# Where the operands of TensorE's matmuls begin in SBUF: weights at multiples of 64 bytes, moving operands 32 bytes past one

## The chip, the cores and the metric

The kernel runs on one core of a Trainium2 chip. The metric is the device time of one execution in microseconds (us): 1510.12 is the median of three runs of the kernel before (1508.47 to 1510.69). The profile is of one further execution, which took 1509.39 us, 1507.2 of them inside the span that the profiler shows.

## The reference

Two stages run one after the other, in float32. The first is an attention over 32 inducing points for each of 4 batches of 12416 tokens with 128 channels; the second is a gated feed-forward layer (SwiGLU) with 1536 hidden units over all 49664 tokens.

```
def mab(q, kv):
    s = scale * (q @ kv.transpose(0, 2, 1))
    a = softmax(s)                      # with 1e-9 in the divisor
    return a @ kv
h = mab(I, x)                           # I: the inducing points, for each batch
y = mab(x, h)
g = y @ w_gate                          # 128 x 1536
out = (g * sigmoid(g) * (y @ w_val)) @ w_out
```

## The kernel before, in words

Nearly all of the time is the feed-forward layer. Its input y is never formed: y = a @ h, so y @ w_gate = a @ (h @ w_gate), and the 32 rows of h @ w_gate and of h @ w_val are computed once for each batch and kept as the weight tile `tw` (128 partitions x 3072, float32r; the halves of a high-and-low split lie in different groups of 32 partitions). The attention weights a, split and transposed in the same way, are put into a tile `stack` (128 x 512 or 480) by small DMAs on SP's queue.

A batch is 25 column units of 512 or 480 tokens (for each, one `stack`), a unit is 12 slots, and a slot is 128 hidden units. In a slot TensorE runs five matmuls, each with 128 x 128 weights and 512 or 480 moving columns:

- `front`: L670 and L671, weights from `tw`, moving operand `stack`. ScalarE then takes silu of the gate (L673), and VectorE multiplies (L678) into `h`, or in place in PSUM for three slots of twelve.
- `split`: `h_hi` is h rounded to float32r (L687, ScalarE, in one slot of twelve VectorE), `h_lo` is the rest h - h_hi (L689, GpSimd, VectorE in three slots of twelve).
- `back`: L703 (weights `wo_lo`, moving `h_hi`), L704 (`wo_hi`, `h_hi`), L705 (`wo_hi`, `h_lo`), accumulated over the 12 slots of a unit in one PSUM bank.

The first unit of the first batch is an exception: its `back` is one plain float32 matmul (L701) on an unsplit h, which lies in a buffer of the `h_hi` pool; its weights stand in tiles called `s_all`, `tw` and `xn_sb`.

The order of all instructions is written out by hand (lists of steps with the slot at which each runs), so the scheduler moves nothing. The attention of the next batch is spread over the slots of the present one.

What the change touches is where tiles lie. A partition's bytes are handed out in the order in which pools are opened and tiles are named, each tile rounded up to 32 bytes. `stack`, `h_hi` and `h_lo` are allocated with `WF + SKIP` columns (WF = 512), of which 512 are used; they rotate through 3, 11 and 10 buffers. `odd` is a column of 0 and -1, allocated early, ahead of all weights. These are the addresses in the built programs, as the remainder by 64 bytes:

| tile | used as | before | after |
|---|---|---|---|
| `tw`, `wo_hi`, `wo_lo` | weights of L670, L671, L703 to L705 | 32 | 0 |
| `stack`, 3 buffers | moving, L670 and L671 | 32, 0, 32 | 32 |
| `h_hi`, 11 buffers | moving, L703 and L704 | 0, 32, 0, ... (six at 0) | 32 |
| `h_lo`, 10 buffers | moving, L705 | 32, 0, 32, ... (five at 0) | 32 |
| `silu`, `h`, `xn_sb` | ScalarE, VectorE, GpSimd; `xn_sb` moving in L306 | 0 | 32 |
| `xt_sb`, `eT`, `wgv_sb`, `a_hi`, `a_lo` | attention | 32 | 0 |
| `below` | weights of L399 | 0 | 32 |
| `s_all` of batches 0 and 2; of 1 and 3 | attention | 32; 0 (with L701's weights) | 32; 32 |

A weight slice begins a multiple of 512 bytes behind the start of its tile, so the remainder of a tile is that of all its slices.

Of the kernel before, what the change touches and what calls it, by code (L numbers as in the profile page):

```python
# [9 lines left out]
F32 = mybir.dt.float32  # L10
# [8 lines left out]
P = 128  # L19
# [13 lines left out]
NF = len(FC)  # L33
W = 32 * max(CH)
WF = 32 * max(FC)
SKIP = 8
NT = DFF // P
SCALE = 1.0 / math.sqrt(C)

# [70 lines left out]
def induced_set_attention_then_swiglu(ctx: ExitStack, tc: tile.TileContext, xt, xn, ind, wgv, wo, out):  # L110
    nc = tc.nc

    const = ctx.enter_context(tc.tile_pool(name="const", bufs=1))
# [4 lines left out]
    one = ctx.enter_context(tc.tile_pool(name="one", bufs=1))  # L118
# [14 lines left out]
    group = const.tile([P, NG], F32, name="group")  # L133
    nc.vector.tensor_reduce(out=group, in_=ident.rearrange("p (j m) -> p j m", m=M), op=ALU.add, axis=AX.X)

    odd = const.tile([P, 1], F32, name="odd")
    nc.gpsimd.memset(odd, 0.0)
    for j in (1, 3):
        nc.gpsimd.memset(odd[32 * j:32 * j + 32, :], -1.0)
# [59 lines left out]
    def attention(b, one, xn0=None, xt0=None):  # L199
# [266 lines left out]
        def stack(u):  # L466
            if u not in st.stack:
                st.stack[u] = stp.tile([P, WF + SKIP], F32R, name="stack")[:, :WF]
            return st.stack[u]
# [190 lines left out]
    def front(st, b, c, t):  # L660
# [13 lines left out]
        if u.whole:  # L674
            u.h = hip.tile([P, WF + SKIP], F32, name="h_hi")[:, :WF]
        else:
# [4 lines left out]
    def split(u):  # L681
        if u.whole:
            return
        n = u.n
        u.hi = hip.tile([P, WF + SKIP], F32R, name="h_hi")[:, :WF]
        u.lo = lop.tile([P, WF + SKIP], F32R, name="h_lo")[:, :WF]
        (nc.vector.tensor_copy if u.cast_dve else nc.scalar.copy)(out=u.hi[:, :n], in_=u.h[:, :n])  # L687
# [108 lines left out]
```

## Time and profile before

| | |
|---|---|
| median of three runs | 1510.12 us |
| the profiled execution | 1509.39 us |
| its span | 1507.2 us |
| TensorE busy | 1485.9 us (99%) |
| ScalarE busy | 1282.9 us (85%) |
| VectorE busy | 1219.0 us (81%) |
| GpSimd busy | 1207.1 us (80%) |
| matmuls of the five lines | 1200 each of L670 and L671, 1188 each of L703, L704 and L705 |

The granted TensorE clock is 9 of 10 tenths or more in every slice of the page. A busy TensorE is not yet one at its peak: matmuls overlap, and the next begins before the modelled end of the one ahead. The pace is therefore read from how many matmuls begin in a stretch without waits.

### The profile page before, as it was taken

The page shows a single profiled execution, that of the slowest core. Times are in us where ns is not written, and L with a number is a line of the kernel's source. Part 1 is how long each engine was busy: PE and PEld are TensorE (multiplying, and loading weights), DVE is VectorE, ACT ScalarE, POOL GpSimd, SP SyncE. Part 2 cuts the span into 40 slices and gives each one's busy share as a digit, 9 for nine tenths or more (in the row PEclk, how much of TensorE's full clock was granted, in tenths as well). Part 3 has the DMA queues.
Part 4 walks back from the last instruction along what each step waited for, and adds up shares of the span by engine and source line. Part 5 has one row for each costly group of instructions (what it writes and reads, how often), then busy time and mean ns, then how long its engine had stood idle before and what let it go on. Part 6 is the DMA issues. An engine that isn't in the chain of part 4 may idle for free.

```text
span 1507.2 us, 24960 instructions
## 1 busy us (share of the span) xinstructions
PE 1485.9 (99%) x7465; PEld 1167.9 (77%) x7465; DVE 1219.0 (81%) x2083; ACT 1282.9 (85%) x2389; POOL 1207.1 (80%) x995
## 2 busy tenths in 40 slices
PE   8899999999999999999999999999999999999999
PEld 5476777778887776788887777678888887888887
DVE  6788878878888778788888778878878878878877
ACT  4787798789898787889988888789898898898897
POOL 1588767878898778788888877878889888888887
PEclk9999999999999999999999999999999999999999
DMA  9025422222133333121114324221111111111110
GB/s 366 23 93 184 136 86 97 83 59 57 40 108 118 123 125 111 45 66 37 40 44 130 124 85 156 77 67 49 41 40 35 37 40 40 34 40 40 41 40 20
DMA packets 50822, 119.80 MB, mean 79 GB/s; under 512 B 11392, under 2 KB 28288, under 8 KB 50688
## 3 DMA queue, kind: packets, MB, share of 16 engines
q1 hardware_dynamic: 50688, 118.22, 24.6%
q8 instruction: 59, 0.97, 0.3%
q14 instruction: 75, 0.61, 0.1%
HBM read 62.87 MB, written 25.43 MB: 59 GB/s over the span
## 4 chain that ended last, share of the span: by engine, by line
PE 89%; ACT 4%; DVE 2%; POOL 2%; DMA 1%; issue 1%; SPq 0%; DVEq 0%; ACTq 0%; POOLq 0%
PE o L703 17%; PE o L705 17%; PE gv L671 17%; PE gv L670 17%; PE o L704 17%; PE o L258 2%; ACT silu L673 1%; POOL h_lo L689 1%; DMA xt<-xt 1%; ACT h_hi L687 1%; PE o L306 1%; ACT s_all L290 1%; PE o L701 1%; DVE h L678 0%; PE gv L408 0%
## 5 line engine op out<-in xcount | busy, mean ns | idle before, releaser
L689 POOL TENSOR_TENSOR h_lo<-h,h_hi 128x512 fp32r<-128x512 f32 (+1 forms) x890 | 1109.1, 1270 | 249.0 <-ACT h_hi L687 194.5
L673 ACT ACTIVATE silu<-gv 128x512 f32<-128x512 f32 (+1 forms) x1200 | 703.4, 587 | 135.5 <-PE gv L670 91.3
L678 DVE TENSOR_TENSOR h<-gv,silu 128x512 f32<-128x512 f32 (+1 forms) x891 | 594.6, 668 | 209.6 <-ACT silu L673 133.5
L687 ACT CAST h_hi<-h 128x512 fp32r<-128x512 f32 (+1 forms) x788 | 475.4, 603 | 53.4 <-DVE h L678 47.0
L670 PE MATMUL gv<-stack,tw 128*128 128x512 f32 (+1 forms) x1200 | 470.9, 392 | 1.9 <-DMA stack<-a_lo 1.6
L703 PE MATMUL o<-h_hi,wo_lo 128*128 128x512 f32 (+1 forms) x1188 | 467.2, 393 | 3.4 <-DVE ob L712 1.9
L671 PE MATMUL gv<-stack,tw 128*128 128x512 f32 (+1 forms) x1200 | 465.9, 388 | 1.7 <-DVE h L678 0.6
L705 PE MATMUL o<-h_lo,wo_hi 128*128 128x512 f32 (+1 forms) x1188 | 462.8, 390 | 0.2
L704 PE MATMUL o<-h_hi,wo_hi 128*128 128x512 f32 (+1 forms) x1188 | 460.0, 387 | 0.0
L703 PEld LDWEIGHTS o<-h_hi,wo_lo 128*128 128x128 f32 x1188 | 223.1, 188 | 82.9 <-issue 33.9
L671 PEld LDWEIGHTS gv<-stack,tw 128*128 128x128 f32 x1200 | 225.5, 188 | 53.1 <-ACT silu L673 3.7
L670 PEld LDWEIGHTS gv<-stack,tw 128*128 128x128 f32 x1200 | 225.5, 188 | 51.9 <-issue 3.6
L705 PEld LDWEIGHTS o<-h_lo,wo_hi 128*128 128x128 f32 x1188 | 222.9, 188 | 54.1 <-POOL h_lo L689 10.9
L704 PEld LDWEIGHTS o<-h_hi,wo_hi 128*128 128x128 f32 x1188 | 223.2, 188 | 40.9
L678 DVE TENSOR_TENSOR gv<-gv,silu 128x512 f32<-128x512 f32 (+1 forms) x297 | 201.7, 679 | 48.0 <-ACT silu L673 32.7
L689 DVE TENSOR_TENSOR h_lo<-gv,h_hi 128x512 fp32r<-128x512 f32 (+1 forms) x297 | 197.6, 665 | 1.3
L687 ACT CAST h_hi<-gv 128x512 fp32r<-128x512 f32 (+1 forms) x294 | 167.8, 571 | 6.4 <-DVE gv L678 4.1
L712 DVE COPY ob<-o 128x512 f32<-128x512 f32 (+1 forms) x100 | 66.4, 664 | 1.4 <-PE o L705 1.4
L687 DVE CAST h_hi<-h 128x512 fp32r<-128x512 f32 (+1 forms) x103 | 49.7, 483 | 0.0
L464 POOL TENSOR_TENSOR a_lo<-aT,a_hi 128x512 fp32r<-128x512 f32 (+2 forms) x27 | 35.0, 1296 | 1.5 <-ACT a_hi L459 1.5
L435 POOL TENSOR_TENSOR s_all<-s_all,mx 128x448 f32<-128x448 f32 (+3 forms) x28 | 27.0, 963 | 0.7 <-DVE mx L431 0.7
L188 POOL TENSOR_TENSOR wgv_sb<-work 128x512 int32<-128x512 int32 x2 | 2.6, 1294 | 29.9 <-DVE work L185 28.7
(159 smaller groups left out, 522.0 us busy)
## 6 DMA issues: line engine op xcount, KB each, us to landing
xt_sb<-xt SPq DMA_DIRECT2D x32, 896.0 KB, 5.0
xn_sb<-xn SPq DMA_DIRECT2D x18, 896.0 KB, 6.2
out<-ob SPq DMA_DIRECT2D x52, 256.0 KB, 2.0
out<-ob SPq DMA_DIRECT2D x48, 240.0 KB, 2.0
stack<-a_hi SPq DMA_DIRECT2D x96, 64.0 KB, 2.0
stack<-a_lo SPq DMA_DIRECT2D x96, 64.0 KB, 2.0
stack<-a_hi SPq DMA_DIRECT2D x96, 60.0 KB, 2.0
stack<-a_lo SPq DMA_DIRECT2D x96, 60.0 KB, 2.0
```

The source lines that it names most:

```text
L258: nc.tensor.matmul(out=ps[32 * j:32 * j + 32, 32 * (lo - b0):32 * (hi - b0)], lhsT=lhsT, rhs=st.xt[q][:, lo - CH0[q]:hi - CH0[q], j, :], s ...
L464: eng.tensor_sub(out=st.al[q][:, :n], in0=st.at[q][:, :n], in1=st.ah[q][:, :n].bitcast(F32))
L670: nc.tensor.matmul(out=u.g[:, :n], lhsT=st.w[:, wcol(0, t)], rhs=rhs, start=True, stop=True)
L671: nc.tensor.matmul(out=u.v[:, :n], lhsT=st.w[:, wcol(1, t)], rhs=rhs, start=True, stop=True)
L673: nc.scalar.activation(out=s[:, :n], in_=u.g[:, :n], func=AF.Silu)
L678: nc.vector.tensor_mul(out=u.h[:, :n], in0=u.v[:, :n], in1=s[:, :n])
L687: (nc.vector.tensor_copy if u.cast_dve else nc.scalar.copy)(out=u.hi[:, :n], in_=u.h[:, :n])
L689: eng.tensor_sub(out=u.lo[:, :n], in0=u.h[:, :n], in1=u.hi[:, :n].bitcast(F32))
L703: nc.tensor.matmul(out=o[:, :n], lhsT=wo_lo[:, ws], rhs=u.hi[:, :n], start=(t == 0), stop=False)
L704: nc.tensor.matmul(out=o[:, :n], lhsT=wo_hi[:, ws], rhs=u.hi[:, :n], start=False, stop=False)
L705: nc.tensor.matmul(out=o[:, :n], lhsT=wo_hi[:, ws], rhs=u.lo[:, :n], start=False, stop=(t == NT - 1))
L712: nc.vector.tensor_copy(out=ob[:, :n], in_=o[:, :n])
```

## The change

`SKIP` goes from 8 to 16 columns, which takes the distance between buffers of `stack`, `h_hi` and `h_lo` from 2080 to 2112 bytes (33 times 64). `odd` is allocated with 16 columns, of which the first is used, so that everything allocated behind it lies 32 bytes further on, counted by the remainder. A tile `gap` of 32 bytes, which nothing reads, is added to the pool ahead of the stacks and zeroed once on GpSimd.

```
-SKIP = 8
+SKIP = 16
...
+    nc.gpsimd.memset(one.tile([P, 8], F32, name="gap"), 0.0)
+
-    odd = const.tile([P, 1], F32, name="odd")
+    odd = const.tile([P, 16], F32, name="odd")[:, :1]
     nc.gpsimd.memset(odd, 0.0)
```

All engines keep their order; GpSimd alone has one instruction more. The beginning of its order before, where `ident` is the identity matrix that TensorE's first transposes need:

```order
6 masks.py:197 MEMSET ident 128x128
7 L137 MEMSET odd 128x1
8 L143 MEMSET half 64x1
9 L144 MEMSET half 64x1
10 masks.py:199 ISA
11 masks.py:199 AFFINE_SELECT ident<-ident 128x128
```

And now, with all line numbers 2 higher behind the added lines:

```order
6 masks.py:197 MEMSET ident 128x128
7 L136 MEMSET gap 128x8
8 L139 MEMSET odd 128x1
9 L145 MEMSET half 64x1
10 L146 MEMSET half 64x1
11 masks.py:199 ISA
12 masks.py:199 AFFINE_SELECT ident<-ident 128x128
```

The memset of `gap` stands ahead of the instruction that finishes `ident`; nothing else has moved.

## Rows read from the trace of the kernel before

**Rows 1.** The page: span, then busy time, share and count of two engines.

```profile
span 1507.2 us, 24960 instructions
PE 1485.9 (99%) x7465; PEld 1167.9 (77%) x7465; DVE 1219.0 (81%) x2083; ACT 1282.9 (85%) x2389; POOL 1207.1 (80%) x995
```

**Rows 2.** Busy time by windows, all engines: stretch, length, busy (count), clock, DMA.

```profile
core 0: us, PE busy (x) PEld busy (x) DVE busy (x) ACT busy (x) POOL busy (x), PEclk, DMA share, GB/s
1160.00:1300.00 140.00, 139.99 (x604) 112.53 (x603) 113.44 (x181) 125.43 (x232) 120.55 (x95) 1.00 0.13 38
1380.00:1440.00 60.00, 59.98 (x276) 51.15 (x275) 49.49 (x84) 53.94 (x106) 52.11 (x45) 1.00 0.13 38
```

**Rows 3.** The page's groups by line: count, busy us, mean ns, idle before.

```profile
L670 PE MATMUL gv<-stack,tw 128*128 128x512 f32 (+1 forms) x1200 | 470.9, 392 | 1.9 <-DMA stack<-a_lo 1.6
L703 PE MATMUL o<-h_hi,wo_lo 128*128 128x512 f32 (+1 forms) x1188 | 467.2, 393 | 3.4 <-DVE ob L712 1.9
```

**Rows 4.** L670, 480 columns, 16 windows of 12 each: stack buffers 1, 2, 3.

```profile
sum 202.36, PE 72.69; mean PE 4.54
...
sum 202.52, PE 72.88; mean PE 4.56
...
sum 209.41, PE 72.74; mean PE 4.55
```

**Rows 5.** L703, 480 columns, 190 windows of one each: h_hi at 0, at 32.

```profile
sum 79.90, PE 72.27; mean PE 0.38
...
sum 79.68, PE 72.02; mean PE 0.38
```

**Rows 6.** L703, 512 columns, 190 windows of one each: h_hi at 0, at 32.

```profile
sum 82.65, PE 75.05; mean PE 0.39
...
sum 82.25, PE 74.69; mean PE 0.39
```

**Rows 7.** L705, 512 columns, 190 windows of one each: h_lo at 0, at 32.

```profile
sum 82.57, PE 74.97; mean PE 0.39
...
sum 82.30, PE 74.75; mean PE 0.39
```

**Rows 8.** Timeline, 1350 us: start, length, instruction (PEld is the weight load).

```profile
1350.28 0.37 PE L670 MATMUL gv<-stack,tw 128*128 128x480 f32 x1
1350.28 0.19 PEld L671 LDWEIGHTS gv<-stack,tw 128*128 128x128 f32 x1
...
1350.49 0.38 PE L671 MATMUL gv<-stack,tw 128*128 128x480 f32 x1
```

**Rows 9.** L671 ahead of L701, four windows each: next weights at 0, at 32.

```profile
sum 1.68, PE 1.58; mean PE 0.39
...
sum 1.69, PE 1.57; mean PE 0.39
```

**Rows 10.** Timeline of TensorE: two of those eight L671, with the L701 behind.

```profile
58.65 0.39 PE L671 MATMUL gv<-stack,tw 128*128 128x512 f32 x1
58.89 1.02 PE L701 MATMUL o<-h_hi,s_all 128*128 128x512 f32 x2
...
59.97 0.39 PE L671 MATMUL gv<-stack,tw 128*128 128x512 f32 x1
60.20 1.02 PE L701 MATMUL o<-h_hi,tw 128*128 128x512 f32 x2
```

**Rows 11.** ScalarE's L687 from h, 480 columns, 130 windows: h_hi at 0, at 32.

```profile
sum 79.25, ACT 76.66; mean ACT 0.59
...
sum 79.37, ACT 76.69; mean ACT 0.59
```

**Rows 12.** Timeline of the start.

```profile
0.88 0.10 POOL L137 MEMSET odd<- 128x1 f32 x1
...
1.24 0.29 POOL masks.py:199 TENSOR_SCALAR_AFFINE_SELECT ident<-ident 128x128 f32<-128x128 f32 x1
```

**Rows 13.** Chain that ended last, first 22 us: shares by line.

```profile
by line: DMA xt<-xt 72.2%; SPq L226 16.6%; PE gv L258 3.9%; issue 2.5%; SPq L147 1.7%
```

## The prediction

> **What bounds the kernel now.** I read the page first. TensorE is busy 1485.9 of 1507.2 us and every other engine 85% or less [rows 1]. Then I cut out two stretches of the last batch, where nothing runs but the five matmuls of each slot. TensorE has no gap in them (139.99 of 140.00 us and 59.98 of 60.00), and the granted clock is 1.00, the 2.4 GHz level, so there is neither a wait nor a lower clock to win [rows 2]. ScalarE, the next engine, is busy 125.43 of 140 us, or 90%. In such stretches the time is the number of matmuls times their spacing: 140 us / 604 = 231.8 ns for 512 columns, 60 us / 276 = 217.4 ns for 480. At one column per cycle of 2.4 GHz 512 columns would take 213.3 ns, so some 18 ns of each matmul are something else. The two spacings differ by 14.4 ns for 32 columns, 0.45 ns a column where a cycle is 0.417: much of the 18 ns grows with the columns, which belongs to the moving stream and not to the load of the weights (a count is good to half a matmul, so no finer split is read from it).
>
> There are 2 x 1200 + 3 x 1188 = 5964 of these matmuls [rows 3]. One ns on each is 6.0 us of the total, 0.4%. This change moves no work, so only such a nanosecond can move the time. A difference of 0.2%, 3.0 us, is about what a measurement of this kernel can tell from none.
>
> **What the moving operand's start costs now.** The kernel before has both starts in it, because its buffers lie 2080 bytes apart: the same line reads buffers that begin at a multiple of 64 and buffers that begin 32 bytes past one. So I summed one line's durations by buffer.
>
> - `stack`, L670 with 480 columns: 192 matmuls on each buffer take 72.69 us on the first (at 32), 72.88 on the second (at 0), 72.74 on the third (at 32) [rows 4]. Per matmul: (72.88 - 72.715) / 192 = 0.86 ns more at 0.
> - `h_hi`, L703: 190 matmuls take 72.27 us at 0 and 72.02 at 32 with 480 columns, 1.3 ns each [rows 5]; 75.05 and 74.69 with 512 columns, 1.9 ns [rows 6].
> - `h_lo`, L705 with 512 columns: 74.97 and 74.75, 1.2 ns [rows 7].
>
> Every pair has the same sign: a moving operand that begins 32 bytes past a multiple of 64 is the faster one, by 0.86 to 1.9 ns. Ends of matmuls are modelled and the next one begins about 160 ns ahead of them, so not all of such a difference need come back in the start of the next. I take 1.0 ns, near the stack's price.
>
> **The change part by part.**
>
> - *`SKIP` 16, moving operands all at 32.* Now at 0 are one stack buffer of three (33 of the 100 units, 24 matmuls each: 792), six of eleven `h_hi` buffers (1188 x 2 x 6/11 = 1296) and half of the `h_lo` buffers (594): 2682 of 5964. At 1.0 ns these give back 2.7 us, at the lower price 2.3, at the row-by-row prices (0.86, 1.6 as the middle of 1.3 and 1.9, 1.2) 0.7 + 2.1 + 0.7 = 3.5. Nothing hides them, since TensorE is the bound; ScalarE at 90% does not become one by 0.2%.
> - *`odd` wider, weights at 0 instead of 32.* All weights of the five lines lie at 32 now, so no row of them has the new value. The weights of the next matmul are read beside the running one: both begin at 1350.28, and the load takes 0.19 us of the 0.21 to the next start [rows 8]. The nearest rows are eight L671 of the first unit, moving operand at 32, while L701's weights are loaded beside them, four times from tiles at 0 and four times from one at 32. The four with weights at 0 sum to 1.58 us, the others to 1.57 [rows 9]; the next start comes 0.24 us later in the first pair, 0.23 in the second [rows 10]. So weights at 0 are no gain that shows, and no loss beyond 2.5 ns a matmul (10 ns, the step of the print, over four). Those two ends are -2.5 and +2.5 ns, or 15 us either way on 5964; I take 0, which the rows are nearest to, and keep the ends for the range.
> - *Other engines' operands.* `silu`, `h` and part of the `h_hi` and `h_lo` buffers move to 32. ScalarE writes 130 `h_hi` at 0 in 76.66 us and at 32 in 76.69 [rows 11]: nothing, and beside a TensorE that is never idle there. If this cover were gone and the 0.2 ns real, its 788 casts would cost 0.2 us.
> - *`gap`.* One memset like that of `odd`, 0.10 us, ahead of the instruction that finishes `ident` at 1.24 us [rows 12]. TensorE's warm-up begins up to 0.1 us later, but the chain of the first 22 us is the loads of x, 72.2% of it DMA and 16.6% their issue [rows 13]. I count 0; 0.1 us if the cover is not there. The loads of x now land at 0 instead of 32; they bound these 22 us, so a slower landing would be seen, but I have no row for its price and put it between -0.3 and +0.3 us, 2% of 16.
>
> Sum, on the profiled execution: 1509.39 - 2.7 = 1506.7 us. That execution is 0.7 us under the median of the runs, so I forecast 1510.1 - 2.7 = 1507.4. Its own range, from the prices above and the half us of the start, is 1506 to 1509.
>
> **Rules of the Trainium skill.** The spread between buffers says that a start counts, if little [rows 4 to 7]. The Trainium skill's page "SBUF — State Buffer", section Specifications, says that SBUF has lines of 16 bytes and that full speed takes two hits on a line. All starts here, before and after, are multiples of 16, so by this rule the time would stay 1510.1; the trace disagrees by about 1 ns a matmul. Its page "TensorE: Matmul & The Clock Gate", section Step-by-step, says that loading the next weights does not take read bandwidth from the running matmul. By that rule the weights' start counts nothing and the sum stays at -2.7; rows 9 agree to within their 2.5 ns.
>
> **The rivals.**
>
> 1. *It is the distance that counts, not the start (slower).* In the kernel before the fast matmuls are those whose moving operand and weights, read at the same time, have the same remainder (32 and 32), and the slow ones those where they differ by 32. The rows of the five lines fit this just as well, since all weights are at 32. After the change all differ by 32: the 3282 that are fast today become slow, +3.3 us at 1.0 ns, 1513.4. It decides from a price of 3.0 / 3282 = 0.92 ns on. For it: the 1.58 against 1.57 us of rows 9 has its sign, and 2.5 ns is within reach of 1.0. Against it: four matmuls are few.
> 2. *Weights at 0 are better in themselves (much faster).* A slice of 512 bytes that begins at a multiple of 64 touches fewer pieces of 64 bytes, and the load beside the stream disturbs it less. With half of the 2.5 ns bound, 1.25 x 5964 = 7.5 us more: 1500. Against it: rows 9 show no gain.
> 3. *The change doesn't act.* The difference between buffers is one of the modelled ends and not of starts; then nothing moves: 1510.1.
> 4. *Weights at 0 are worse in themselves*, by over 1.25 ns: 1515 and more. Only rows 9 speak of it, with the right sign and the weight of four instructions.
>
> **How the numbers follow.** Forecast 0.38, rival 1 0.25, rival 2 0.20, rival 3 0.12, rival 4 0.05. The forecast lies close to the bound of 0.2% (1507.1), so half of it counts as faster: 0.19 + 0.20 = 0.39. Of rival 1 seven tenths are beyond the bound: 0.175 + 0.05 = 0.225 slower. The rest, 0.385, is the same. The range leaves out the lower half of rival 2 and rival 4: 1499 to 1514.5.
>
> **What the next profile would show.** If the forecast holds, the three stack buffers take the same 72.7 us for 192 matmuls, the spacing is 231.3 ns in the 512-column stretch and 217 in the 480-column one (45% of 1.0 ns less), and idle time of TensorE is as before. Rival 1 shows 232.4 ns and L703 at 72.3 us for 190; rival 2 less than 230.6. Rival 3 shows shorter L703 rows at an unchanged count in rows 2's stretches. The forecast is wrong in its basis if the spacing moves by more than 2 ns either way, or if waits of TensorE on another engine appear in the last batch.

## The result: slower by 0.3%, and the profile after

The changed kernel takes 1513.91 us (median of 8 runs, 1512.20 to 1515.92), the kernel before 1509.91 us on the same chip (8 runs, 1505.88 to 1510.92). The ratio is 1.0032, with a 95% interval of 1.0022 to 1.0041: slower by some 4 to 5 us, where 2.7 us faster was forecast. The time lies in the range, the sign is wrong. The profiled execution took 1514.92 us.

The page of the changed kernel; its line numbers are 2 higher than before:

```profile
span 1512.8 us, 24961 instructions
PE 1492.5 (99%) x7465; PEld 1168.8 (77%) x7465; DVE 1219.9 (81%) x2083; ACT 1283.4 (85%) x2389; POOL 1211.0 (80%) x996
```

The span has grown by 5.6 us and TensorE's busy time by 6.6, against [rows 1]; its idle time has not grown (20.3 us against 21.3). So no wait has come, the matmuls themselves are slower. The best measure is how many begin in one long stretch, taken behind the start of the kernel, since the length of that start varies between executions. Busy time of TensorE in that stretch, first of the kernel before, then of the changed one:

```profile
200.00:1450.00 1250.00, 1246.48 (x6138) 1.00 0.23 70
```

```profile
200.00:1450.00 1250.00, 1246.70 (x6118) 1.00 0.23 70
...
1160.00:1300.00 140.00, 140.00 (x603) 1.00 0.13 40
1380.00:1440.00 60.00, 60.00 (x274) 1.00 0.14 40
```

At an unchanged granted clock 20 matmuls fewer begin, 20 x 0.23 = 4.6 us. The stretches of [rows 2] hold 603 instead of 604 and 274 instead of 276. From the starts in the trace, averaged over all pairs of successive matmuls of the five lines without a wait between them (5611 pairs before, 5613 after), the spacing went from 231.89 to 233.06 ns with 512 columns and from 217.68 to 218.36 with 480: 0.93 ns on the average pair.

The same windows as in [rows 4 to 7] show which matmuls lost. L672 (the old L670) on the three stack buffers; then L705 (the old L703) with 480 and with 512 columns, and L707 (the old L705) with 512, 190 windows each; all moving operands now begin at 32:

```profile
sum 203.50, PE 73.02; mean PE 4.56
...
sum 202.91, PE 73.08; mean PE 4.57
...
sum 209.86, PE 73.12; mean PE 4.57
...
sum 79.89, PE 72.22; mean PE 0.38
...
sum 82.53, PE 75.05; mean PE 0.40
...
sum 82.63, PE 75.07; mean PE 0.40
```

The buffers are alike, as the change intends. But they are alike at the slow value: on L672 even the least, 73.02, is above the 72.88 of the slow buffer before [rows 4]; the other three read 72.22 beside the 72.27 that a start at 0 took before and not the 72.02 of a start at 32 [rows 5], 75.05 beside 75.05 and 74.69 [rows 6], 75.07 beside 74.97 and 74.75 [rows 7]. A start at 32 is no longer fast. What it was compared with has moved: the weights.

### The profile page after: what moved, and what is told of

The parts are those of the page before. It is cut to its first block, busy times and chain, and to the rows that moved or that the text cites. A ratio compares the mean times of both kernels' runs of the same rounds, so it can differ in the third digit from the quotient of the medians.

```text
span 1512.8 us, 24961 instructions
## 1 busy us (share of the span) xinstructions
PE 1492.5 (99%) x7465; PEld 1168.8 (77%) x7465; DVE 1219.9 (81%) x2083; ACT 1283.4 (85%) x2389; POOL 1211.0 (80%) x996
## 4 chain that ended last, share of the span: by engine, by line
PE 88%; ACT 2%; DVE 1%; issue 1%; POOL 1%; DMA 0%; SPq 0%; DVEq 0%; ACTq 0%
PE o L705 17%; PE o L707 17%; PE gv L672 17%; PE gv L673 17%; PE o L706 17%; PE o L260 2%; PE o L308 1%; ACT silu L675 1%; POOL h_lo L691 0%; DVE h L680 0%; ACT s_all L292 0%; ACT h_hi L689 0%; DMA stack<-a_lo 0%; PE gv L410 0%; PE gv L260 0%
## 5 line engine op out<-in xcount | busy, mean ns | idle before, releaser
L672 PE MATMUL gv<-stack,tw 128*128 128x512 f32 (+1 forms) x1200 | 472.4, 394 | 2.1 <-DMA stack<-a_lo 1.9
L705 PE MATMUL o<-h_hi,wo_lo 128*128 128x512 f32 (+1 forms) x1188 | 468.3, 394 | 3.3 <-DVE ob L714 1.8
L707 PE MATMUL o<-h_lo,wo_hi 128*128 128x512 f32 (+1 forms) x1188 | 464.2, 391 | 0.2
L705 PEld LDWEIGHTS o<-h_hi,wo_lo 128*128 128x128 f32 x1188 | 223.0, 188 | 84.8 <-issue 34.6
L672 PEld LDWEIGHTS gv<-stack,tw 128*128 128x128 f32 x1200 | 225.5, 188 | 52.8 <-issue 6.1
L707 PEld LDWEIGHTS o<-h_lo,wo_hi 128*128 128x128 f32 x1188 | 223.3, 188 | 54.7 <-POOL h_lo L691 10.6
L453 POOL TENSOR_TENSOR s_all<-s_all,sm 128x512 f32<-128x512 f32 (+2 forms) x27 | 25.8, 956 | 0.4 <-DVE sm L449 0.4
```

What stands on the lines that cost most here:

```text
L672: nc.tensor.matmul(out=u.g[:, :n], lhsT=st.w[:, wcol(0, t)], rhs=rhs, start=True, stop=True)
L705: nc.tensor.matmul(out=o[:, :n], lhsT=wo_lo[:, ws], rhs=u.hi[:, :n], start=(t == 0), stop=False)
L707: nc.tensor.matmul(out=o[:, :n], lhsT=wo_hi[:, ws], rhs=u.lo[:, :n], start=False, stop=(t == NT - 1))
```

## Experiments

Two theories. *Distance*: a matmul is slow when the starts of its moving operand and of weights read at the same time differ by 32 bytes modulo 64. *Starts*: each operand has a price for its own start, whatever the other's. A third, *layout*, says that any new placement shifts the time by chance. The first four runs fill the square of the two starts, and mix them. "Spacing" below is the mean over the same kind of pairs of a run's trace, about 5600, less that of the kernel before, with a standard error of some 0.06 ns.

**Weights at 32, moving operands at 32.**

```
-SKIP = 8
+SKIP = 16
```

> SKIP 16 alone: weights stay at 32 past a multiple of 64, and all moving operands stand at 32 as well (distance 0). Distance theory (a matmul is slow when its moving operand and the weights read beside it differ by 32 modulo 64): all matmuls go to the fast kind, 2682 x 1.0 ns = -2.7 us against before (ratio 0.998), 190 of L703 with 480 columns sum to 72.0 us and with 512 to 74.7. Starts theory (a moving operand at 0 costs 1.0 ns, weights at 0 cost 1.4 ns, each by itself): the same -2.7 us. Layout theory (the starts do nothing, any new layout is some us slower or faster by chance): no better than the changed kernel, about 1.003.

1507.32 us, ratio 0.9994 (0.9986 to 1.0003); spacing -0.32 ns. Count in the long stretch, then 190 of L703 with 480 and with 512 columns:

```profile
200.00:1450.00 1250.00, 1246.30 (x6141) 1.00 0.23 70
...
sum 79.67, PE 72.11; mean PE 0.38
...
sum 82.34, PE 74.75; mean PE 0.39
```

The matmuls are of the fast kind. The gain is 1 us rather than the 2.7 expected, and within the noise of no change; the spacing itself accounts for 0.32 x 5964 = 1.9 us.

**Weights at 0, moving operands at 0.**

```
-SKIP = 8
+SKIP = 16
...
-    odd = const.tile([P, 1], F32, name="odd")
+    odd = const.tile([P, 16], F32, name="odd")[:, :1]
```

> SKIP 16 and the wide odd, no gap: weights at 0 and all moving operands at 0 (distance 0). Distance theory: all fast, -2.7 us against before (0.998), L703 sums 72.0 (480 columns) and 74.7 us (512). Starts theory: both prices on every matmul, 1.9 ns over before on 5964, +11.5 us (1.0076), L703 sums 72.4 and 75.3 us. Layout theory: about 1.003.

1508.43 us, ratio 0.9999 (0.9988 to 1.0009); spacing -0.33 ns.

```profile
200.00:1450.00 1250.00, 1246.33 (x6143) 1.00 0.23 70
...
sum 79.61, PE 72.09; mean PE 0.38
...
sum 82.30, PE 74.73; mean PE 0.39
```

This decides between distance and starts. Starts at 0 on both sides, each slow by the starts theory, give the same times as 32 on both sides; that theory asked for 1.0076. The distance theory's own 0.998 did not come either: its matmuls are of the fast kind, but no gain in the time shows.

**Weights at 32, moving operands at 0.**

```
-SKIP = 8
+SKIP = 16
...
+    nc.gpsimd.memset(one.tile([P, 8], F32, name="gap"), 0.0)
```

> SKIP 16 and the gap, odd as before: weights at 32, all moving operands at 0 (distance 32, the mirror of the changed kernel). Distance theory: all slow, +3.3 to +5.5 us against before (1.002 to 1.0037), L703 sums 72.25 and 75.05 us. Starts theory: 3282 matmuls lose 1.0 ns, +3.3 us (1.0022). Layout theory: about 1.003. This one tells whether weights at 0 have a price of their own, by its distance to the changed kernel (1.0032).

1514.18 us, ratio 1.0033 (1.0021 to 1.0045); spacing +0.92 ns, the changed kernel's +0.93.

```profile
200.00:1450.00 1250.00, 1246.69 (x6119) 1.00 0.23 70
...
sum 79.74, PE 72.20; mean PE 0.38
...
sum 82.64, PE 75.04; mean PE 0.39
```

The mirror image costs the same as the change, so weights at 0 have no price of their own. The layout theory is out as well: of four new layouts the two with distance 0 stand at 0.9994 and 0.9999, the two with distance 32 at 1.0032 and 1.0033.

**Which weights: one mixed layout, then a pair that moves `h_lo` alone.** In the mixed one `odd` is wide and a tile of 32 bytes stands ahead of `tw`:

```
-SKIP = 8
+SKIP = 16
...
+    nc.gpsimd.memset(xtp.tile([P, 8], F32, name="gap", bufs=1), 0.0)
```

> wo_hi and wo_lo at 0, tw at 32, all moving operands at 32. It tells which weights count, those of the running matmul or those of the next, which are loaded beside it. If the next: L670 (beside it a slice of tw is loaded) and L705 (tw again) are fast, L671, L703 and L704 (wo_lo, wo_hi, wo_hi) are slow. If its own: L670 and L671 fast, L703, L704 and L705 slow. So L671 and L705 decide: with 512 columns 190 of L705 sum to 74.75 if fast, 75.07 us if slow; 192 of L670 with 480 columns to 72.7 in both cases, of L671 to 72.8 or 73.05. The total is the same by both, three of five lines slow: 3/5 of the way between the first and the changed kernel, about 1.001.

1510.70 us, ratio 1.0010 (1.0000 to 1.0020), as expected. The lines did not separate the theories by themselves: the spacing of L671 was +0.72 ns, slow, as "next" has it, but L705 was at -0.10, between fast and slow. So the pair puts `h_hi` at 0 in both, and `h_lo` at 0 in the first (its edit below) and at 32 in the second:

```
-        u.lo = lop.tile([P, WF + SKIP], F32R, name="h_lo")[:, :WF]
+        u.lo = lop.tile([P, WF + SKIP], F32R, name="h_lo")[:, 8:8 + WF]
```

> wo_hi and wo_lo at 0, tw and stack at 32, h_hi at 0, h_lo at 0: of L705 the own weights (wo_hi) have the remainder of its moving operand, the next ones (tw, loaded beside it) differ by 32. If the next count alone, L705 is slow here (190 with 512 columns sum to 75.05 us) and fast in its twin; if the own alone, the reverse (74.7 here). If both count half, no difference.

> The twin: h_lo at 32, all else the same. Of L705 the own weights differ by 32, the next have its remainder. Next alone: fast, 74.7 us for 190; own alone: slow, 75.05; both by half: as its twin.

One execution of each (1506.81 and 1510.09 us); 190 of `h_lo`'s matmul with 512 columns, own weights at its remainder and next ones 32 apart:

```profile
sum 82.50, PE 75.00; mean PE 0.39
```

and the twin, own weights 32 apart and next ones at its remainder:

```profile
sum 82.18, PE 74.66; mean PE 0.39
```

The spacing says the same: +0.26 against -0.85 ns (1063 and 1061 pairs, error 0.10). So on its own line `h_lo`'s matmul goes with the weights of the next one, those loaded beside it [rows 8]. But the matmul behind it gives most of that back: the spacing of L670, for which no address differs between the twins, is -1.07 ns in the first and -0.24 in the second. Over all pairs the twins stand at -0.19 and -0.25 ns (error 0.06), where next weights alone would put the first 1.1 x 1188 / 5964 = 0.22 ns above the second. So the total does not show whether the next weights alone count, and that stays open, as does why L705 of the mixed layout was only half fast.

**Distance 64 and distance 96.** In the traces so far the remainder of the distance by 128 had shown as well.

```
-SKIP = 8
+SKIP = 32
+OFF = 16
...
-            st.stack[u] = stp.tile([P, WF + SKIP], F32R, name="stack")[:, :WF]
+            st.stack[u] = stp.tile([P, WF + SKIP], F32R, name="stack")[:, OFF:OFF + WF]
```

`h_hi` and `h_lo` are sliced in the same way; the second kernel has `OFF = 24`.

> SKIP 32 (buffers 2176 bytes apart, 17 times 128) and the slice of 512 columns begins 16 columns into each buffer: every moving operand 64 bytes past the remainder of the weights, modulo 128. Distance theory in its finer form (the remainder by 128 counts: in the five traces so far the spacing against the mean of before was about -0.1 ns at distance 0, +0.65 at 32, -0.6 at 64, +1.25 at 96): -0.6 x 5964 = -3.6 us, ratio 0.9976. Distance theory modulo 64 only: like the first experiment, 0.9995. Layout theory (any of these differences is chance): anywhere from 0.999 to 1.003.

> The same with the slice 24 columns into each buffer: distance 96 modulo 128 everywhere. Finer distance theory: +1.25 x 5964 = +7.5 us, ratio 1.005. Modulo 64 only: like the changed kernel, 1.0032. Starts theory (moving operands at 0 cost 1.0 ns, weights at 32 nothing): +3.3 us, 1.0022.

Distance 64: 1506.61 us, ratio 0.9987 (0.9977 to 0.9996), spacing -0.76 ns.

```profile
200.00:1450.00 1250.00, 1246.08 (x6149) 1.00 0.23 70
...
L706 PEld LDWEIGHTS o<-h_lo,wo_hi 128*128 128x128 f32 x1188 | 223.4, 188 | 53.8 <-POOL h_lo L690 11.7
```

Distance 96: 1516.15 us, ratio 1.0045 (1.0030 to 1.0059), spacing +1.35 ns.

```profile
200.00:1450.00 1250.00, 1246.73 (x6112) 1.00 0.23 70
...
L706 PEld LDWEIGHTS o<-h_lo,wo_hi 128*128 128x128 f32 x1188 | 223.3, 188 | 54.2 <-POOL h_lo L690 9.9
```

The spacings lie outside the modulo-64 values (-0.3 and +0.9) on either side; the ratios alone would not tell, as their intervals hold those values too. The difference in spacing alone, 2.11 ns x 5964, asks for 12.6 us between them; the counts give 37 x 0.23 = 8.5 and the ratios 8.7. Part of it is handed back: the group shown behind each count is the weight load of `h_lo`'s matmul, and the time for which it sat waiting for GpSimd's `h_lo` is 11.7 us at the faster pace and 9.9 at the slower. That is 1.8 of some 4 us; the rest is not accounted for.

**Sixteen starts in one kernel.** `h_hi` and `h_lo` of successive slots begin 0, 8, ... 120 bytes into their buffers, with the buffers at the remainder of the weights.

```
+        d = 2 * (next(turn) % 16)
-        u.hi = hip.tile([P, WF + SKIP], F32R, name="h_hi")[:, :WF]
+        u.hi = hip.tile([P, WF + SKIP], F32R, name="h_hi")[:, d:d + WF]
```

> One look for its trace. SKIP 32, buffers all at the remainder of the weights by 128; h_hi and h_lo of one slot after the other begin 0, 8, 16, ... 120 bytes into their buffers, 16 starts in turn. If lines of 64 or 128 bytes are fetched and the two streams meet at their edges, the duration of L704 is a step function of the start, low around 0 and 64, high around 32 and 96, with the steps at multiples of 16 or 32 bytes. If only starts off 64 bytes count by themselves, it is flat but for 0 and 64. 130 of L704 should differ by about 0.15 to 0.25 us between the best and the worst start.

Spacing of L703 to L705 against the mean of before, some 200 pairs for each start, error 0.2 ns: at 0, 16, 32, ... 112 bytes -0.2, -0.2, +0.7, -0.7, -1.0, -0.4, +1.2, +0.7. At the odd multiples of 8 from 8 to 120: +1.6, +0.6, +0.6, -0.2, +0.9, +1.0, +1.5, +1.9. Low at 0 and 64 and high at 32 and 96, as expected, but no clean step, and of the odd multiples of 8 all but one are slow. The mean spacing, +0.26 ns, asks for 1.5 us more than before; the one execution took 1506.9 us, about 1 us less than the median of before. That alone would be noise, but it led on: GpSimd's subtraction had become faster in some slots, 1037 ns instead of 1235 with 480 columns, wherever `h_hi` and `h_lo` began 8 bytes past a multiple of 16 and `h` did not.

**`h` 8 bytes off.** Distance 64 as above; `h`, which TensorE never reads, is moved by 8 bytes, and in a control by 16 (slice from 4). The larger tile shifts the buffers behind it, so `h_hi` and `h_lo` are sliced from column 24 in both.

```
-            u.h = u.v if t in DVE_TILES else hp.tile([P, WF], F32, name="h")
+            u.h = u.v if t in DVE_TILES else hp.tile([P, WF + 8], F32, name="h")[:, 2:2 + WF]
```

> All moving operands at distance 64, and the tile h, which TensorE does not read, begins 8 bytes into its buffer. In the sweep GpSimd's subtraction took 1037 ns where h_hi and h_lo began 8 bytes past a multiple of 16 and h did not, 1237 elsewhere, and TensorE waited 4 us less than in before. If a difference of 8 bytes between the operands of GpSimd is enough, its mean for 480 columns falls from 1238 to about 1040 ns here too, at no price on TensorE: the waits of some 4 us go on top of the -2.8 us of distance 64, ratio about 0.9955. If it is the place of the result that counts, GpSimd stays at 1238 ns and the ratio at 0.9987.

> The same with h 16 bytes into its buffer, the control: by either reading of the sweep GpSimd stays at about 1238 ns and the ratio at 0.9987, as in the experiment with distance 64 alone.

The control: 1506.52 us, ratio 0.9989 (0.9979 to 0.9998).

```profile
L690 POOL TENSOR_TENSOR h_lo<-h,h_hi 128x480 fp32r<-128x480 f32 x431 | 520.8, 1232 | 88.2 <-ACT h_hi L688 69.5 <-PE o L705 11.3 <-DVE h_hi L688 5.5
...
L706 PEld LDWEIGHTS o<-h_lo,wo_hi 128*128 128x128 f32 x1188 | 223.3, 188 | 53.0 <-POOL h_lo L690 11.1
```

With 8 bytes: 1496.30 us, ratio 0.9921 (0.9907 to 0.9934).

```profile
L690 POOL TENSOR_TENSOR h_lo<-h,h_hi 128x480 fp32r<-128x480 f32 x431 | 443.7, 1040 | 162.0 <-ACT h_hi L688 127.1 <-PE o L705 15.9 <-DVE h_hi L688 7.3
...
L706 PEld LDWEIGHTS o<-h_lo,wo_hi 128*128 128x128 f32 x1188 | 223.2, 188 | 43.0
```

GpSimd takes 1040 ns instead of 1232, the weight load no longer waits for it, and against the control 10 us go, where some 4 were expected (against the kernel before 12, where 7 were). The spacing is -0.77 and -0.74 ns, so TensorE's own pace has no part in the difference of the two. The move has a price elsewhere: VectorE's casts of `h` to `h_hi`, 48 of them with 480 columns, take 671 ns instead of 443. This version beats the kernel before by 12 us and, by the two ratios, the changed one by some 17.

## Why the prediction was wrong

- *What bounds the kernel, and what a nanosecond is worth*: right. TensorE stayed at 99%, no new wait came, and the change shows in the spacing.
- *What the moving operand's start costs*: the price was right, its owner wrong. In the trace of before the two kinds of pairs lie 0.99 ns apart (-0.45 ns at 32, +0.54 at 0), the 1.0 that was taken. But rows 4 to 7 vary the moving start while all weights of the five lines stand at 32. In such rows "begins at 32" and "begins where the weights do" are one and the same, and the sum took the first.
- *The step that failed* is "`odd` wider, weights at 0 instead of 32 ... I take 0". As a price of the weights' own start 0 was right (the mirror image costs the same). As the other half of a distance it turned all 3282 fast matmuls into slow ones, and the 2682 that were to become fast stayed slow. Rival 1 said this, at 1513.4 us against 1513.9 measured, which is nearer than its sum deserves: the spacing asks for 0.93 x 5964 = 5.5 us, not 3.3. More pairs now stand at distance 96, the worst one (2558 of 5613, against 955 of 5611 before), but at the prices of before (+0.32 ns at 32, +0.90 at 96) the new mix makes only 0.58 ns. The same distances cost more in the changed kernel (+0.66 and +1.24), and why is open: the distance modulo 128 is not the whole of it.
- *Rows 9* were the only ones off that diagonal, with weights at 0 beside a moving operand at 32. Their sign was right (1.58 against 1.57 us), their number was four. The bound drawn from them was misread: two printed sums 10 ns apart can differ by 0 to 20, which is no gain and up to 5 ns a matmul of loss, and not 2.5 either way. In whole ns the trace has the next matmul 234, 231, 233 and 235 ns behind these L671 with weights at 0, and 228, 234, 228 and 234 with weights at 32: 2.25 ns more at 0, with an error of 1.9, for rival 1 but not clear of noise. By all other rows rival 1 and the forecast stood level, so 0.38 against 0.25 had no ground.
- *The rule of the Trainium skill* that loading the next weights takes no read bandwidth from the running matmul ("TensorE: Matmul & The Clock Gate", Step-by-step) supported the forecast. The runs disagree: moving of the two operands the weights alone by 32 bytes, from the first experiment to the changed kernel, cost 1.25 ns on the mean pair. On its own line the pair of `h_lo` disagrees too, by 1.1 ns in 232.
- *Other engines, `gap` and the loads of x* at nothing: right as far as the trace shows. ScalarE is busy 1283.4 us against 1282.9, GpSimd 1211.0 against 1207.1, TensorE waits 1.6 us for `ident` in both, and the slowest load of x lands after 14.1 us against 15.9.

## What to carry to other kernels

When two things are read side by side, rows in which only one of them varies cannot tell its own price from the distance between the two; look for the row off the diagonal before the sum, or let the two readings stand level. An engine that is 99% busy can still be paced by another: the wait stood in the row of the weight loads and not in that of the matmuls. In a kernel bound by float32r matmuls like these, keep the moving operands off a distance of 32 or 96 bytes modulo 128 from the weights: 64 was the best tried, and between it and 96 lay 0.6% of the time. And try other starts for operands that TensorE doesn't read, for the sake of the engines that do; here that gave 0.7%.

## What the runs showed of the hardware

- The spacing of these float32r matmuls depends on the distance between the starts of the moving operand and of the weights, and not on either start by itself: -0.76 ns at 64 bytes modulo 128, -0.3 at 0 and 64 mixed, +0.9 at 32 and 96 mixed, +1.35 at 96. In these runs the own and the next weights stand at the same remainder. How the two reads meet was not shown, and other things shift single rows by as much.
- GpSimd's subtraction of two operands in SBUF took 1040 ns with 480 columns when its first operand began 8 bytes off the others modulo 16, and 1232 when all three began at multiples of 16. In the sweep the result moved along with the second operand; whether all three or only two must differ was not tried, nor why.
